# Loading a 512x512 channel weight in 8 KB runs, with every fourth channel in the transposes

## The chip, the cores and the metric

The kernel runs on one core of a Trainium2 chip. The metric is device time in microseconds (us). Profiles have their own zero; the profiled executions are about 1.8 us shorter than the times, because the time covers more than the profiled span.

## The reference, cut to what matters

Eight batches of 576 rows pass through a sliding-window attention, then through a spectral layer: the first 64 modes of a real Fourier transform along the sequence are each multiplied by a complex 512x512 weight (`w_r`, `w_i`), transformed back to `y`, and one channel weight `w_ch` closes the layer.

```python
u = x + y                                  # y: 64 spectral modes, each through its own weights
return (u + np.maximum(u @ w_ch, 0.0)).astype(np.float32)
```

The 127 mode matrices used and `w_ch` are 1 MB each in fp32.

## The kernel before, where the change touches it

GpSimd issues all loads of weights. Mode weights are read with four rows of a matrix in one partition (8 KB contiguous in memory) and become bf16 on the way; the channel weight is read with one row per run (2 KB) and stays 4 bytes wide. So channel `128*c + p` of the channel weight sits in partition `p`, and everything multiplied with it is transposed in packed blocks of 128 channels.

```python
def load_w(i, pool, tag, wt=None):                       # a mode weight: 8 KB runs
    ...
    nc.gpsimd.dma_start(out=wt, in_=src[m].rearrange("(p c) e -> p c e", c=NC))
...
            if m == 6:                                   # the channel weight: 2 KB runs
                nc.gpsimd.dma_start(out=wch, in_=moe_w_ch.rearrange("(c p) e -> p c e", p=128))
...
def channel(i):                                          # x @ w_ch, between modes
    ...
    for c in range(NC):
        nc.tensor.transpose(out=pst[:, c, :], in_=x_sb[:, b, t + k, 128 * c:128 * c + 128],
                            identity=ident_bf)           # in_ is the stationary side (a weight load)
    ...
    for c in range(NC):
        nc.tensor.matmul(out=psz, lhsT=xT[:, c, :], rhs=wch[:, c, :], ...)
...
def last_mode(m, w, im, c0, c1):                         # the last four modes: 16 loads per matrix
    for c in range(c0, c1):
        for e in range(NC):
            nc.tensor.matmul(out=view(psl, ...), lhsT=w[:, c, 128 * e:128 * e + 128], rhs=xq(...), ...)
...
        for m in range(ME + 2, NM):                      # ME = NM - 4
            for im in range(2):
                idle(1, 2)                               # filler matmuls, results unused
                last(m, im)                              # last_mode once its weight has landed
        idle(0, 2)
```

After the last of them, two VectorE copies take `psl` into `YT2`, which is multiplied with `wch` and transposed (`psw`, `psa`); then the output rows are formed.

The softmax here doesn't subtract the row's maximum and nothing guards it: scores larger than these inputs give would overflow.

## Time and profile before

| | before |
|---|---|
| time, median of 4 runs | 426.12 us (426.09 to 426.28) |
| profiled span | 424.3 us |
| last weight has landed | 389.4 us |
| tail after it | 34.9 us |
| DMA packets | 28166 |
| channel weight: issue to landing; first use | 148.95 to 167.8 us; 210.5 us |

The DMA share of a stretch is the busy time of the 16 DMA engines over their time; 1.06 means that packets on an engine overlap a little, and is what a full queue looks like here. "PEclk" is the clock granted to TensorE, as a share of full speed.

Two groups of PE weight loads (minimum, median and maximum in ns, then first and last start), from the views of lines 614 and 793 of the kernel before:

```profile
L614 PEld LDWEIGHTS <-x_sb x144: 95/98/151, 137.6 to 294.5; 128*128 128x128 bf16 x144
L793 PEld LDWEIGHTS <-wt x80: 95/98/103, 374.3 to 389.9; 128*128 128x128 bf16 x80
```

Packed loads of 128 bf16 columns take 98 ns, both for the transposes of x and for the last modes.

### The profile page before, as it was taken

The page shows a single profiled execution, that of the slowest core. Times are in us where ns is not written, and L with a number is a line of the kernel's source. Part 1 is how long each engine was busy: PE and PEld are TensorE (multiplying, and loading weights), DVE is VectorE, ACT ScalarE, POOL GpSimd, SP SyncE. Part 2 cuts the span into 40 slices and gives each one's busy share as a digit, 9 for nine tenths or more (in the row PEclk, how much of TensorE's full clock was granted, in tenths as well). Part 3 has the DMA queues.
Part 4 walks back from the last instruction along what each step waited for, and adds up shares of the span by engine and source line. Part 5 has one row for each costly group of instructions (what it writes and reads, how often), then busy time and mean ns, then how long its engine had stood idle before and what let it go on. Part 6 is the DMA issues. An engine that isn't in the chain of part 4 may idle for free.

```text
span 424.3 us, 8788 instructions
## 1 busy us (share of the span) xinstructions
PE 348.0 (82%) x3772; PEld 215.7 (51%) x3772; DVE 184.5 (43%) x397; ACT 171.2 (40%) x314; POOL 78.9 (19%) x141
## 2 busy tenths in 40 slices
PE   6999999999988897363698977977569997588993
PEld 5665665666665564122365644554324443255682
DVE  6466765766673211061443413331103433240994
ACT  4585866866763310021032312122203333130993
POOL 7131221331022222012111011211111113200000
PEclk9999999999996899556599999999968999999998
DMA  8999999999999999999999999999999999994598
GB/s 142 212 213 212 212 216 211 214 213 211 215 213 214 215 212 261 214 216 212 215 216 213 215 215 214 215 214 213 216 213 214 214 213 214 213 214 96 194 387 329
DMA packets 28166, 91.98 MB, mean 217 GB/s; under 512 B 2352, under 2 KB 2608, under 8 KB 28128
## 3 DMA queue, kind: packets, MB, share of 16 engines
q0 software_dynamic: 24864, 81.80, 96.6%
q1 hardware_dynamic: 3120, 9.50, 5.9%
q8 instruction: 29, 0.48, 0.4%
q10 hardware_dynamic: 144, 0.13, 0.1%
q14 instruction: 9, 0.07, 0.0%
HBM read 162.53 MB, written 9.44 MB: 405 GB/s over the span
## 4 chain that ended last, share of the span: by engine, by line
PE 38%; DMA 37%; issue 12%; DVE 8%; POOL 2%; ACT 2%; POOLq 0%; DVEq 0%
DMA wt<-in_moe_w_r_dram 23%; DMA wt<-in_moe_w_i_dram 14%; PE pso L324 7%; PE pst L226 6%; PE psy L592 4%; PE pso L903 4%; PE psv L243 3%; DVE x_sb L332 3%; PE psw L742 3%; PE pss L280 2%; PE pss L381 2%; PE psx L346 2%; PE pss L299 2%; DVE vT L59 2%; POOL wt L122 1%
## 5 line engine op out<-in xcount | busy, mean ns | idle before, releaser
L592 PE MATMUL psy<-wt,XQ 128*32 128x512 bf16 (+1 forms) x404 | 86.1, 427 | 42.6 <-DMA wt<-in_moe_w_i_dram 25.6
L592 PEld LDWEIGHTS <-XQ 128*32 128x32 bf16 (+1 forms) x476 | 46.2, 132 | 82.7 <-issue 65.8
L621 DVE CAST xT<-pxt 128x256 fp32r<-128x256 bf16 (+1 forms) x68 | 26.0, 434 | 56.4 <-PE pxt L614 41.1
L628 ACT CAST Z<-psz 128x512 fp32r<-128x512 f32 x36 | 21.1, 587 | 58.4 <-PE psz L626 58.1
L305 ACT ACTIVATE et<-pss 128x512 bf16<-128x512 f32 x72 | 39.2, 599 | 12.8 <-PE pss L299 12.8
L626 PE MATMUL psz<-wch,xT 128*128 128x512 f32 x144 | 40.3, 417 | 0.4 <-DVE xT L621 0.4
L324 PE MATMUL pso<-vt,et 128*64 128x65 bf16 (+1 forms) x576 | 34.0, 209 | 5.2 <-DVE x_sb L332 5.1
L324 PEld LDWEIGHTS <-et 128*64 128x64 bf16 (+1 forms) x576 | 23.7, 113 | 17.2 <-issue 9.8
L626 PEld LDWEIGHTS psz<-wch,xT 128*128 128x128 f32 x144 | 26.1, 193 | 11.6 <-issue 5.7
L59 DVE COPY x_sb<-psy 128x256 f32<-128x256 f32 x15 | 6.4, 424 | 56.4 <-PE psy L592 56.4
L58 ACT COPY x_sb<-psy 128x256 f32<-128x256 f32 x15 | 5.6, 373 | 60.6 <-DVE x_sb L59 60.6
L332 DVE TENSOR_TENSOR x_sb<-pso,rcp 128x640 bf16<-128x640 f32 x32 | 26.3, 823 | 0.9
L122 POOL DMA_DIRECT2D wt<-in_moe_w_r_dram x15 | 10.7, 713 | 77.7 <-PE psy L592 68.7
L903 PE MATMUL pso<-Y,trigI 128*128 128x512 f32 x80 | 23.1, 403 | 0.1
L926 DVE TENSOR_TENSOR ot<-pso,x_sb 128x512 f32<-128x512 f32 x35 | 22.2, 685 | 1.5 <-PE pso L903 1.1
L280 PE MATMUL pss<-band,ident_bf 64*64 64x512 bf16 x136 | 20.4, 407 | 1.5 <-ACT et L305 1.5
L59 DVE COPY vT<-pst 128x768 bf16<-128x768 bf16 x16 | 15.3, 958 | 13.0 <-PE pst L226 13.0
L117 POOL DMA_DIRECT2D wt<-in_moe_w_r_dram x25 | 13.6, 544 | 37.9 <-PE psy L592 22.8
L59 DVE CAST x_sb<-psj 128x512 bf16<-128x512 f32 x18 | 12.2, 688 | 18.5 <-PE psj L804 15.6
L908 ACT ACTIVATE pso<-pso 128x512 f32<-128x512 f32 x36 | 19.2, 594 | 0.0
L58 ACT CAST x_sb<-psj 128x512 bf16<-128x512 f32 x18 | 10.5, 586 | 19.3 <-PE psj L804 19.2
L122 POOL DMA_DIRECT2D wt<-in_moe_w_i_dram x15 | 10.7, 714 | 36.1 <-PE psy L592 35.1
(159 smaller groups left out, 530.3 us busy)
## 6 DMA issues: line engine op xcount, KB each, us to landing
wt<-in_moe_w_r_dram POOLq DMA_DIRECT2D x15, 1024.0 KB, 23.0
wt<-in_moe_w_i_dram POOLq DMA_DIRECT2D x15, 1024.0 KB, 25.4
wt<-in_moe_w_r_dram POOLq DMA_DIRECT2D x25, 512.0 KB, 16.9
wt<-in_moe_w_i_dram POOLq DMA_DIRECT2D x21, 512.0 KB, 18.2
out_dram<-ot SPq DMA_DIRECT2D x15, 512.0 KB, 4.2
rk<-in_k_dram POOLq DMA_DIRECT2D x8, 576.0 KB, 10.5
rq<-in_q_dram POOLq DMA_DIRECT2D x8, 576.0 KB, 14.2
rv<-in_v_dram POOLq DMA_DIRECT2D x8, 576.0 KB, 13.0
```

The costliest lines, as they stand in the source:

```text
L59: return nc.vector.tensor_copy(out=o, in_=i)
L122: nc.gpsimd.dma_start(out=wt, in_=src[m:m + 2].rearrange("m (p c) e -> p m c e", c=NC))
L226: nc.tensor.transpose(out=ps[64 * hh:64 * hh + 64, c, :], in_=src[:, hh, (c0 + c) * D:(c0 + c + 1) * D], identity=ident_bf)
L280: nc.tensor.matmul(out=pss[(2 * w + hh) % 3][64 * half:64 * half + 64, :], lhsT=ident_bf[pp, pp], rhs=view(band[pp], 128 * half, [[0, WIN ...
L305: nc.scalar.activation(out=et[:, hh, :], in_=pss[(2 * w + hh) % 3], func=ACT_F.Exp, scale=EX_SCALE)
L324: nc.tensor.matmul(out=pso[po, hh, (i // 2) * VW:(i // 2) * VW + D + 1], lhsT=et[pk, hh, col:col + 64], rhs=vt[pk, 1 - f % 2, 2 * hh + g / ...
L332: nc.vector.tensor_tensor(out=view(x_sb, b * NT * DM + g * D, [[4 * D, 2], [DM, NT], [1, D]]), in0=view(pso, 0, [[512, 2], [VW, NT], [1, D]]),
L592: nc.tensor.matmul(out=psy[r0:r0 + k, :], lhsT=xq(c, m, im, [[NM, k]]), rhs=w[:, c, :], start=(im + c == 0), stop=(im == (m > 0) and c == ...
L621: nc.vector.tensor_copy(out=xT[:, :, w * k:w * k + w], in_=view(psts[k], j, [[128, NC], [n, w]] if n > 1 else [[128, NC], [1, 64], [64, 2]]))
L626: nc.tensor.matmul(out=psz, lhsT=xT[:, c, :], rhs=wch[:, c, :], start=(c == 0), stop=(c == NC - 1))
L903: nc.tensor.matmul(out=tps[n], lhsT=trigI[:, tr:tr + 128], rhs=pair_tile(what, bb), start=False, stop=stop and r0 + k == 128, skip_group_c ...
L926: nc.vector.tensor_tensor(out=ot[:, j], in0=ps, in1=x_sb[:, b, t, :], op=ALU.add)
```

## The change

The intent is to give the channel weight's load the mode weights' shape, 128 runs of 8 KB instead of 512 of 2 KB. Partition `p` then holds rows `4p` to `4p+3`, and all that meets the weight must take channels `4p+c`: the transposes of x and the weight loads of the last modes read columns at a step of 4, and copies out of PSUM put spectra into and out of that order.

```diff
-            evac(half[h], ps[:, 256 * h:256 * h + 256], h)
+            evac(half[h], view(ps, 2 * h, [[1, 2], [NC, 128]]), h)
...
-                    nc.tensor.transpose(out=pst[:, c, :], in_=x_sb[:, b, t + k, 128 * c:128 * c + 128],
+                    nc.tensor.transpose(out=pst[:, c, :], in_=view(x_sb, (b * NT + t + k) * DM + c, [[NC, 128]]),
...
-                nc.gpsimd.dma_start(out=wch, in_=moe_w_ch.rearrange("(c p) e -> p c e", p=128))
+                nc.gpsimd.dma_start(out=wch, in_=moe_w_ch.rearrange("(p c) e -> p c e", c=NC))
...
+    def by_channel(psa):
+        return view(psa, 0, [[1, 128], [128, NC]])
...
-        nc.vector.tensor_copy(out=pair_tile("Yb", b)[:E0], in_=psa[:E0].rearrange("p c e -> p (c e)"))
+        nc.vector.tensor_copy(out=pair_tile("Yb", b)[:E0], in_=by_channel(psa[:E0]))
...
-                                 lhsT=w[:, c, 128 * e:128 * e + 128],
+                                 lhsT=view(w, c * DM + e, [[NC, 128]]),
... (three more copies out of psa, through by_channel)
```

More of the change, by code (lines that the diff above doesn't have):

```diff
@@ L847, in middle_rows @@
                 nc.vector.tensor_copy(out=pair_tile("Yb", b0 + i)[E0:],
-                                      in_=psa[R * i:R * i + R].rearrange("p c e -> p (c e)"))
+                                      in_=by_channel(psa[R * i:R * i + R]))
                 nc.scalar.copy(out=pair_tile("yw", b0 + i)[E0:], in_=psw[R * i:R * i + R, :])
@@ L886 @@
         lay(EARLY_ROWS)
-        flat = psa.rearrange("p c e -> p (c e)")
         yl = yp.tile([128, 2, DM], FP32R, name="yl")
@@ L895 @@
             nc.scalar.copy(out=pair_tile("yw", b)[E0:], in_=psw[R * b:R * b + R])
-            nc.vector.tensor_copy(out=pair_tile("Yb", b)[E0:], in_=flat[R * b:R * b + R])
-        nc.vector.tensor_copy(out=yl[0:NR, 1], in_=flat[0:NR])
+            nc.vector.tensor_copy(out=pair_tile("Yb", b)[E0:], in_=by_channel(psa[R * b:R * b + R]))
+        nc.vector.tensor_copy(out=yl[0:NR, 1], in_=by_channel(psa[0:NR]))
         def add(n, what, stop):
```

## The prediction

> **What bounds the kernel now.** I read the page first, from its 40 slices: before any engine I wanted to know whether the transfers ever rest.
>
> ```profile
> PE   6999999999988897363698977977569997588993
> ...
> DMA  8999999999999999999999999999999999994598
> ```
>
> PE has holes (3, 6, 3, 6 in slices 17 to 20, 5 and 6 in slices 29 and 30) while the DMA row stands at 9 from the second slice to the 36th. So I asked for the stretches between the stages, with the DMA share as the column before the last and GB/s as the last.
>
> ```profile
> 5.00:141.00 136.00, 127.44 (x2491) 85.76 (x2489) 85.28 (x152) 87.47 (x146) 34.26 (x60) 0.96 1.09 213
> 141.00:158.00 17.00, 15.18 (x117) 9.54 (x116) 2.32 (x6) 5.02 (x11) 4.46 (x7) 1.00 1.07 214
> 158.00:170.00 12.00, 9.08 (x63) 5.43 (x63) 1.53 (x5) 1.54 (x5) 2.61 (x6) 1.00 1.10 255
> 170.00:350.00 180.00, 138.20 (x715) 77.49 (x714) 56.30 (x164) 41.20 (x85) 26.85 (x43) 0.87 1.06 214
> 350.00:385.00 35.00, 25.70 (x212) 13.99 (x209) 10.83 (x19) 8.53 (x17) 6.88 (x13) 1.00 1.06 212
> 385.00:390.00 5.00, 4.18 (x68) 2.75 (x65) 0.00 (x0) 0.00 (x0) 0.00 (x0) 1.00 0.37 74
> ```
>
> The share never falls below 1.06 before 385 us (over 1 because packets on one DMA engine overlap a little), and the rate stays at 212 to 214 GB/s, except at 158 to 170 us. That exception is the transfer this change touches: the channel weight is written as fp32, so as many bytes arrive as are read, while each mode weight is read as fp32 and written as bf16. The third view is the chain that ended last, where the stream stops.
>
> ```profile
> 371.13 18.30 DMA wt<-in_moe_w_i_dram
> 389.43 0.05 issue
> 389.48 0.64 PE psl L793 x16
> 390.14 0.23 DVE YT L880
> 390.37 0.28 DVE YT L882
> 390.64 0.14 issue
> 390.77 1.17 PE psw L742 x4
> ```
>
> The last load is issued 18.3 us before it lands, so the queue is that deep and engine waits behind it do not starve it. The end is then two terms: the time the DMA engines need to push every byte (to 389.4 us), and the tail after it (424.3 - 389.4 = 34.9 us). A change counts only if it alters DMA work before the last weight, or tail work after it.
>
> **What the Trainium skill says.** "DMA: Bandwidth & Descriptors", section "Why small descriptors are slow (HBM only)", gives a fixed cost for each packet; by its 3 cycles beside 32-byte beats a 2 KB packet would lose 3 of 67 cycles, an 8 KB one 3 of 259, an estimate of 3% between them. This trace agrees in kind and shows more, as worked out below. "TensorE: Matmul & The Clock Gate", section "Weight-path perf modes", says that the fast weight load is taken for 128 non-fp32 weights, with its columns "packed or strided", for column steps of up to about a thousand elements. A step of 4 would keep it; the trace of before has no strided 128-column bf16 load, so nothing confirms this yet. "SBUF — State Buffer", section "Door 1: The DMA port swizzle", says that up to 8 bf16 elements may be stepped over for free; the trace has a step of 2 only: the 64-column loads of ident_bf at line 804 take 109 ns against 110 ns for packed 64-column loads at line 226. "VectorE: DVE Perf Modes", section "Why PSUM operands drop a tier", puts fp32 out of PSUM at one element per cycle[...]. The trace agrees: the copies into YT read PSUM at a step of 32 elements in runs of 4 and take 288 ns for 128 elements, and the packed 512-element copy takes 687 ns. The difference, 399 ns for 384 elements, is 1.04 ns each, so the stride costs nothing seen.
>
> **The change, part by part.**
>
> Instructions. Apart from line numbers, the instruction streams of the two kernels agree on every engine in number, order and size. One row differs in shape: the load of the channel weight is 128 rows of 2048 elements, not 128x4x512. There is nothing to gain or lose by count.
>
> The load. Before, it is 512 packets of 2 KB; after, 128 of 8 KB. What one costs now comes from the DMA engines' time. Two stretches of 12 us, that with the load (158 to 170 us) first, then a plain one (178 to 190 us):
>
> ```profile
> DMA packets 1046, 3.06 MB, mean 255 GB/s; under 512 B 47, under 2 KB 47, under 8 KB 1044
> ...
> q0 software_dynamic: 1044, 3.04, 109.4%
> ...
> DMA packets 667, 2.57 MB, mean 214 GB/s; under 512 B 40, under 2 KB 40, under 8 KB 667
> ...
> q0 software_dynamic: 667, 2.57, 106.2%
> ```
>
> In the plain stretch 667 - 40 = 627 packets of 4 KB written (8 KB read) fill 12 us on 16 engines: 192 / 627 = 306 ns each, so a mode weight of 128 packets costs 128 x 306 / 16 = 2.45 us. In the other, 1044 - 47 = 997 data packets; 512 are the channel weight's, the other 485 are mode packets and take 485 x 306 = 148.4 of the 192 us. That leaves 43.6 us for 512 packets, 85 ns each, so the channel weight costs 512 x 85 / 16 = 2.72 us. If an 8 KB packet of it costs what the mode weights' 8 KB reads do, it becomes 2.45 us: **0.27 us less**. The trace's own packet durations, which contain the overlap, bound this from above: 99 ns for a 2 KB packet against 324 ns for one that reads 8 KB, so 4 x 99 - 324 = 72 ns per 8 KB, times 128 / 16 = 0.58 us, over a share of 1.06 some 0.54 us. The bytes are the same, so no more than a few tenths can be had. As the stream has no gap, what is saved moves the last landing forward by as much. I take 0.3 us.
>
> The weight's arrival. Its first use is at 210.5 us and it lands at 167.8 us, so arriving earlier is worth nothing, and only the freed DMA time counts. GpSimd's issue took 757 ns; it sat idle for 3.5 us after it, so a shorter issue buys nothing.
>
> The transposes of x (line 614, 144 weight loads at 98 ns, 210 to 295 us). Their columns now step by 4 elements. If the fast load survives, nothing changes. If it is lost, I size it from the other loads: 16-column to 64-column bf16 loads take 111 and 110 ns, and 128 columns take only 98, so the 128-column load is the fast kind. In the tail its pairs start 0.51 - 0.10 over 15 gaps = 27 ns apart. A plain load's slope, from the fp32 transposes of line 744, is 132 - 110 = 22 ns for 32 columns, 0.69, or by the pass with 128 columns 140 - 110 = 30 ns for 64, 0.47 ns a column; 128 columns at 0.47 make 60 ns apart, some 30 ns more each. 144 x 30 = 4.3 us of PE time over 85 us, in a stage where the DMA queue holds 20 us of issued loads, and PE waits for mode weights 41.5 us over the kernel: hidden.
>
> The last modes (line 793, 128 weight loads). Same step of 4. Seven of the eight groups of 16 end before the next weight lands (PE waits 0.4 us ahead of the last). The eighth starts when the last weight has landed, on the chain: it costs nothing if the fast load stays, 16 x 30 = **0.5 us if it is lost**. I give the loss one chance in four: 0.1 us expected.
>
> The copies (the spectrum copies on VectorE, 687 ns each, and the copies of psy, 424 ns on VectorE and 373 on ScalarE) read PSUM at steps of 128 and of 4 elements. ScalarE's copy into Xs already reads at a step of 4: 593 against 586 ns packed. In the tail three such VectorE copies stand beside ScalarE's; I expect 0 to 0.05 us.
>
> Sum: 426.12 - 0.3 + 0.1 = 425.9 us.
>
> **The rivals.** (1) Strided weight loads lose the fast kind: for it, no strided 128-column bf16 load has been seen here; against it, the skill's sentence. The time would be 426.12 - 0.3 + 0.5 = 426.3. (2) The write side sets the packet: 8 KB written per packet, where mode packets write 4 KB, could run slower, and the saving vanishes: 426.1. Against it: 2 KB both read and written in 85 ns already moves 24 GB/s per engine, close to the 8 KB / 306 ns = 27 GB/s of the mode reads. (3) PSUM reads at a 512-byte step are slower than at the 128 bytes seen: three copies of 0.69 us in the tail, even 20% slower, add 0.4 us, so 426.2. (4) The strided PE work of 210 to 295 us delays the issues so much that the queue runs dry: it would need a slip of some 20 us, and I found at most 4.3. (5) The transfer is hidden and its saving lost: the unbroken DMA row speaks against it.
>
> **Range and chances.** All rivals lie within half a microsecond of 426. Three runs of before spread by 0.2 us; another chip and another phase of the PE clock can add some tenths. So 425.2 to 426.6 us. Two per cent is 8.5 us, and no term comes near it: within 2% with a chance of 0.98.
>
> **What would show it right or wrong.** The DMA packet count should fall by 384, to some 27780; the 12 us stretch with the load should hold more bytes than 3.06 MB; the last mode weight should land some 0.3 us earlier relative to the start. Lines 614 and 793 should keep weight loads of 98 ns; about 130 ns would mean rival 1. The spectrum copies should stay at 687 ns, and the tail at 34.9 us. I am wrong if the landing moves later, if the queue shows a gap, or if the tail grows by over half a microsecond.

## The result, and the profile after

The changed kernel takes 426.03 us in the median of 4 runs (425.91, 426.01, 426.05 and 427.64). Ratios here are the mean time of one kernel's fast runs over the mean of the other's in the same rounds, so they are not quite the ratio of the quoted medians. This one is 1.0006 (95% interval 0.9982 to 1.003): the one run of 427.64 carries it above 1. The profiled spans are 424.3 us for both. The result is "the same" at 2%, and the measurement cannot see a tenth of a microsecond.

From the page of the changed kernel, the slices and the packets:

```profile
PE   6989998998998899364698977977568986589993
...
DMA  8999999999999999999999999999999999994598
...
DMA packets 27782, 91.98 MB, mean 217 GB/s; under 512 B 2352, under 2 KB 2608, under 8 KB 27616
```

There are 384 packets less, the bytes are the same, and the DMA row is the same slice for slice. The transfers of the changed kernel from 158 to 170 us, the stretch with the load:

```profile
DMA packets 677, 3.10 MB, mean 259 GB/s; under 512 B 48, under 2 KB 48, under 8 KB 548
```

In the same 12 us 3.10 MB arrive, not 3.06. The chain that ended last of the changed kernel (start, duration, what):

```profile
371.48 17.87 DMA wt<-in_moe_w_i_dram
389.34 0.05 issue
389.39 0.72 PE psl L796 x16
390.11 0.02 issue
390.14 0.22 DVE YT L883
```

The last weight lands 0.09 us earlier (389.34 against 389.43), the 16 weight loads and matmuls behind it take 0.72 instead of 0.64 us, and the VectorE copy starts at 390.14 us in both kernels. In these two profiles the gain is given back to the hundredth. The reason for the 0.08 us is in the weight loads:

```profile
L614 PEld LDWEIGHTS <-x_sb x144: 110/113/147, 138.7 to 294.3; 128*128 128x128 bf16 x144
...
L796 PEld LDWEIGHTS <-wt x80: 112/117/147, 375.9 to 389.9; 128*128 128x128 bf16 x80
```

113 and 117 ns, where packed columns took 98. The copies out of PSUM did not change: the eight spectrum copies have a median of 687 ns in both, the copies of psy 425 ns on VectorE and 373 against 372 on ScalarE.

Because the last landing wanders by a tenth from one profile to the next, I also took from the packet records of the traces when the last packet of the n-th mode weight ended, just ahead of the channel weight's packets (mode weight 35) and just behind them (41), always less the same time in the kernel before. What a kernel gains between the two columns lies in the stretch with that load:

| kernel | channel weight in | at weight 35 | at weight 41 | step across the load |
|---|---|---|---|---|
| changed | 8 KB | +0.017 us | -0.137 us | -0.154 us |
| e1 | 8 KB | +0.234 | +0.075 | -0.159 |
| e4 | 8 KB | +0.057 | -0.081 | -0.138 |
| e7 | 8 KB | -0.082 | -0.200 | -0.118 |
| e9 | 8 KB | +1.374 | +1.216 | -0.158 |
| e10 | 8 KB | +0.086 | -0.084 | -0.170 |
| e2 | 2 KB | +0.059 | +0.020 | -0.039 |
| e8 | 2 KB | -0.031 | -0.072 | -0.041 |
| e11 | 2 KB | +0.111 | -0.048 | -0.159 |

The six with 8 KB runs gain 0.15 us on average; the kernel before (0 by definition) and the three others with 2 KB runs gain 0.06. The difference, 0.09 us, is a third of what I had predicted. But e11, with 2 KB runs, gains as much as the kernels with 8 KB, so these steps alone don't settle a tenth; e5 below measures the cost of 2 KB reads on 127 weights at once (0.084 us each). In the landing of the last weight nothing of it can be seen: it is at 389.25 to 389.53 us in the six profiles with 8 KB (mean 389.36) and at 389.22 to 389.43 in the four with 2 KB (mean 389.34). The 0.09 us between the two landings above may be the phase of a run.

### The profile page after: what moved, and what is told of

The parts are those of the page before. It is cut to its first block, busy times and chain, and to the rows that moved or that the text cites. A ratio compares the mean times of both kernels' runs of the same rounds, so it can differ in the third digit from the quotient of the medians.

```text
span 424.3 us, 8778 instructions
## 1 busy us (share of the span) xinstructions
PE 348.6 (82%) x3762; PEld 217.9 (51%) x3772; DVE 184.6 (44%) x397; ACT 171.3 (40%) x314; POOL 78.9 (19%) x141
## 4 chain that ended last, share of the span: by engine, by line
DMA 44%; PE 36%; DVE 8%; issue 7%; ACT 2%; POOL 1%; DVEq 0%; POOLq 0%
DMA wt<-in_moe_w_r_dram 27%; DMA wt<-in_moe_w_i_dram 17%; PE pso L324 7%; PE pst L226 6%; PE psy L592 5%; PE pso L905 4%; PE psv L243 3%; DVE x_sb L332 3%; PE psx L346 3%; PE pss L381 2%; PE pss L280 2%; PE pss L299 2%; DVE vT L59 2%; DVE ot L928 1%; PE pso L790 1%
## 5 line engine op out<-in xcount | busy, mean ns | idle before, releaser
L592 PE MATMUL psy<-wt,XQ 128*32 128x512 bf16 (+1 forms) x404 | 85.0, 428 | 42.9 <-DMA wt<-in_moe_w_i_dram 27.0
L122 POOL DMA_DIRECT2D wt<-in_moe_w_r_dram x15 | 10.7, 715 | 75.5 <-PE psy L592 68.0
```

The costliest lines, as they stand in the source:

```text
L592: nc.tensor.matmul(out=psy[r0:r0 + k, :], lhsT=xq(c, m, im, [[NM, k]]), rhs=w[:, c, :], start=(im + c == 0), stop=(im == (m > 0) and c == ...
```

## The experiments

Theory: two terms of about 0.1 us and opposite sign, cheaper DMA work before the last weight, and strided weight loads behind it; all else is hidden. The rivals are that one or the other is only the phase of a run, that the copies cost, or that PE's extra work in the middle reaches the end. The first three kernels ran five rounds each; the spread of their runs (the kernel before had 425.85 to 429.62 us in 11) turned out too wide for tenths, so what follows from them follows from their traces.

### e1: the load alone

```diff
 # on the kernel before
-  in_=moe_w_ch.rearrange("(c p) e -> p c e", p=128)
+  in_=moe_w_ch.rearrange("(p c) e -> p c e", c=NC)
```

> Kernel before with the channel weight loaded in 8 KB runs and nothing else changed; the result is wrong on purpose. My theory: the load's DMA work alone is the gain, so the last mode weight lands 0.13 us earlier than in the kernel before (as it did in the changed kernel) and the tail stays at 34.9 us: 0.1 to 0.2 us faster, 425.95. Rival A (the earlier landing was the phase of the run and not the load): the same landing as before, 426.1. Rival B (the write of 8 KB per packet is slow): landing later than before.

Measured: 426.35 us against 426.29 in the same rounds, ratio 0.9997 (0.9966 to 1.0027): undecided by time. In the trace the step across the load is -0.159 us, the last weight has landed at 389.34 us against 389.43, and the last 16 matmuls stay at 0.64 us. The theory's landing was 0.13 earlier, it came 0.09 earlier. Rival B, a later landing, falls. Rival A, the phase of the run, does not fall for the landing: e8 and e11, with 2 KB runs, landed earlier still (389.22 and 389.31). And the tail is no constant. In e1 VectorE's copy behind the last group starts 0.09 us earlier than in the kernel before, but its last output ends 0.45 us later: near 411 us a PE weight load waits 0.7 us for a small transfer inside the tail (`Y<-yl`). Nine of the 13 profiles have such a wait (0.2 to 0.7 us); those of the kernel before and of the changed one have none.

### e2: the strides alone

```diff
 # on the changed kernel
-  in_=moe_w_ch.rearrange("(p c) e -> p c e", c=NC)
+  in_=moe_w_ch.rearrange("(c p) e -> p c e", p=128)
```

> Changed kernel with the old load in 2 KB runs; the result is wrong on purpose. My theory: landing as in the kernel before (389.4 us), weight loads of lines 614 and 796 at 113 to 117 ns, the last 16 matmuls 0.72 us instead of 0.63: 0.1 us slower than before, 426.2. Rival C (strided loads cost nothing in the end, since the PE's filler matmuls hide them): equal to before. Rival D (strided copies out of PSUM cost): tail over 35.1 us.

Measured: 426.03 us against 426.29, ratio 0.9987 (0.9963 to 1.001): undecided by time, and not the slower median I expected. In the trace, the landing is at 389.39 us (389.43 before), the weight loads take 113 and 117 ns, the last 16 matmuls 0.73 us, and the copy behind them starts at 390.19 instead of 390.14:

```profile
389.39 0.05 issue
389.44 0.73 PE psl L796 x16
390.17 0.02 issue
390.19 0.23 DVE YT L883
```

So the strides cost their 0.1 us in the chain, against rival C. For rival D the profiled tail (424.5 - 389.4 = 35.1 us) stands at the threshold I had set, but the copies themselves, 687 ns each before and after, show no cost, and a weight load in this tail waits 0.4 us for `Y<-yl`.

### e3: two rows in a partition

```diff
 # on the changed kernel: 4 KB runs, columns at a step of 2
+  out=wch.rearrange("p (h c) e -> p h c e", h=2), in_=moe_w_ch.rearrange("(h p c) e -> p h c e", h=2, c=2)
+  lhsT=view(w, c * DM + 256 * (e // 2) + e % 2, [[2, 128]])     # the transposes and copies likewise
```

> Correct kernel in between: two rows in a partition, 256 packets of 4 KB, columns at a step of 2. From the trace's packet times (99 ns for 2 KB, 325 ns for 8 KB, so 22 ns plus 0.037 ns a byte) a 4 KB packet takes 173 ns, and 256 of them are 2.77 us of one engine's sixteenth against 3.17 and 2.60. My theory: it keeps about two thirds of the saving (0.1 us), and if the cost of a strided weight load grows with the 16-byte lines it touches, a step of 2 costs 105 ns or less, so the tail loses 0.04 us at most: 426.0, best of the three by less than 0.1 us. Rival: the step costs the same 15 ns whatever its size, as soon as columns are not packed: 426.05.

Measured: correct, 426.39 us against 426.29, ratio 0.9989 (0.9966 to 1.0013): not a version that can be said to beat either. (In its profile the last weight has landed at 389.35 us, the last 16 matmuls take 0.66 us, and the copy behind them starts at 390.08, 0.06 us ahead of both kernels; no time confirms it.) What it settles is the stride, at PE's full clock (views of its lines 614 and 797):

```profile
L614 PEld LDWEIGHTS <-x_sb x144: 96/98/151, 137.6 to 294.4; 128*128 128x128 bf16 x144
...
L797 PEld LDWEIGHTS <-wt x80: 96/98/102, 374.2 to 389.8; 128*128 128x128 bf16 x80
```

A step of 2 costs nothing, so the rival "any step but 1" is wrong.

### e4: eight steps, one for each of the last groups

```diff
 # on the changed kernel, by group: steps 2, 3, 4, 5, 8, 6, 16, 1
-  lhsT=view(w, c * DM + e, [[NC, 128]])
+  lhsT=view(w, offset, [[step, 128]])
```

> Changed kernel whose eight last groups of 16 weight loads each read their 128 columns at another step: 2, 3, 4, 5, 8, 6, 16, 1 in this order; the result is wrong on purpose. Theory of lines (each further 16-byte line touched costs): the duration grows with the step up to 8 bf16 (16 bytes) and then stays: about 98 at 1, 103 at 2, 115 at 4, 135 at 8, 135 at 16. Rival (any step but 1[...]): one duration, 113 to 117 ns, at all steps from 2 to 16. Rival 2 (the fast load is lost at some step): a jump to 130 ns or more there.

Measured: 427.79 us in its one run (the output still within the tolerance). The weight loads, in order of time:

```profile
L808 PEld LDWEIGHTS <-wt x16: 113/117/136, 380.3 to 380.8; 128*128 128x128 bf16 x16
...
L813 PEld LDWEIGHTS <-wy x16: 117/130/130, 382.0 to 383.0; 128*128 128x128 bf16 x16
...
L818 PEld LDWEIGHTS <-wy x16: 143/157/166, 384.4 to 385.3; 128*128 128x128 bf16 x16
...
L823 PEld LDWEIGHTS <-wy x16: 125/143/143, 386.8 to 387.4; 128*128 128x128 bf16 x16
...
L828 PEld LDWEIGHTS <-wt x16: 142/168/168, 388.9 to 389.8; 128*128 128x128 bf16 x16
```

These are steps 4, 5, 8, 6 and 16, at PE's full clock: 117, 130, 157, 143 and 168 ns. (Steps 2 and 3 came out at 109 and 110 ns, but the granted clock was 0.50 there; at full clock e3 has 98 for step 2.) The duration grows with the step from 4 up to 8 and little after, as the theory of lines has it, though step 4 is not free and 16 is not equal to 8. There is no jump to a plain load.

The time tells something I had not expected. In this run PE no longer waited for any of the last weights, and the last group started at 391.2 us, 1.8 us later than in the kernel before. (Its weight loads were slower, and PE's clock was 0.50 from 370 to 380 us; the run doesn't separate the two.) PE's work in the last 20 us is a second bound just under the transfers: in the kernel before, the last group waits only 0.43 us for its weight, in the changed one 0.29.

### e5: the same change on 127 weights, the other way round

```diff
 # on the kernel before: all mode weights in 2 KB runs
-  in_=src[m].rearrange("(p c) e -> p c e", c=NC)
+  in_=src[m].rearrange("(c p) e -> p c e", p=128)      # the loads of two modes likewise
```

> Kernel before with all 127 mode weights (not the channel weight) read in 2 KB runs instead of 8 KB: the same change as the one studied, made 127 times and the other way round; the result is wrong on purpose. My theory: one megabyte read in 2 KB runs costs about 0.15 us more DMA time than in 8 KB runs, and the stream has no gap, so 127 x 0.15 = 19 us more (15 to 23): 445 us. Rival (the packet size costs nothing and the 0.15 us between the traces is phase): 426. Rival 2 (descriptor making on GpSimd, now four times as many, becomes the bound): gaps in the DMA row and more than 450 us.

Measured: 436.77 us against 426.08, ratio 1.025 (1.0234 to 1.0265). The last weight landed 10.7 us later too (400.12 us against 389.43). The 10.7 us divided by 127 are 0.084 us a megabyte: for a cost spread over the whole stream the sign and the one-to-one passage are settled, but the size is below my 0.15 and far below the 0.27 of the prediction. (The mode weights are written as bf16, in packets of 1 KB here, so on the write side this is not the channel weight's case.) Rival 2 falls: DMA stays full (page), and a plain 12 us, from 178 to 190 us, has

```profile
DMA packets 2466, 2.49 MB, mean 207 GB/s; under 512 B 37, under 2 KB 2466, under 8 KB 2466
```

2466 - 37 = 2429 data packets in 192 us of DMA engines are 79.0 ns each, so 316 ns for four of them, against the 306 of an 8 KB read: 10 ns x 128 / 16 = 0.08 us a weight. The direct count and the time agree.

### e6: a quarter of the load

```diff
 # on the kernel before
+  nc.gpsimd.dma_start(out=wch[:, 0, :], in_=moe_w_ch[0:128, :])
+  for c in range(1, NC):
+      nc.vector.tensor_copy(out=wch[:, c, :], in_=wch[:, 0, :])
```

> Kernel before that loads only the first 128 rows of the channel weight (128 packets of 2 KB) and fills the rest by three VectorE copies at a time when VectorE is idle; the result is wrong on purpose. My theory: all DMA work before the last weight passes into the end one to one, so three quarters of the 2.6 us fall away: 2.0 us faster, 424.2. Rival (the load hides in slack, or PE takes over as the bound near the end): under 1 us faster.

Measured: 424.61 us against 426.08, ratio 0.9962 (0.9947 to 0.9977): 1.5 us faster, between theory and rival. The trace takes it apart. Across the load the stream gains 1.92 us (from +0.87 at weight 35 to -1.05 at 41), as the theory had it. Ahead of the load it had lost 0.87 us: the issue of the mode weights ahead came 3.7 us later than before (149.85 against 146.18 us), and the DMA share from 150 to 158 us was 1.01 instead of 1.07. Most of that loss did not reach the end: the last weight landed 1.73 us earlier, at 387.70 us. Its group started only at 388.00, because PE was not done with the work ahead: 0.25 us of the gain (0.30 us from landing to start, where the kernel before has 0.05) went to PE, which the rival had said.

### e7: the transposes twice

```diff
 # on the changed kernel
-  for c in range(NC):
+  for c in [i % NC for i in range(2 * NC)]:
```

> Changed kernel with each of the 144 transposes of x made twice into the same place (correct result): some 144 x 60 ns = 8 us more PE work between 138 and 294 us, several times what slower weight loads add there. My theory: hidden behind the DMA stream, time within 0.3 us of the changed kernel, 426.1. Rival (PE's stage from 210 to 285 us, busy for 87%, passes its delay on through the issues of later loads): 2 to 8 us slower.

Measured: correct, 427.77 us against 426.08, ratio 1.0045 (1.0017 to 1.0073). That is not hidden, and my theory seems wrong; but the last weight landed 0.12 us earlier than before, so the loads were not delayed. The lost time is behind, in two parts. PE's clock was 0.50 from 370 to 375 us and 0.54 to 380, and PE then worked without a pause until its last group at 389.90 us, half a microsecond late; VectorE's last output is late by the same (it ends at 419.14 us, 418.68 in the changed kernel). The other 1.5 us come after the last computation: the profile ends 7.1 us behind it, where the other 12 profiles end 5.4 to 5.8 us behind. Only output is written there, and the cause isn't shown. The changed kernel's own profile shows the same stretch of low clock, and just catches up. Stretches of both (columns: busy time of PE, its weight loads, VectorE, ScalarE, GpSimd; then PEclk, DMA share, GB/s), first the kernel before, then the changed one:

```profile
370.00:375.00 5.00, 3.78 (x33) 2.48 (x32) 1.52 (x4) 1.46 (x4) 0.53 (x1) 1.00 1.05 211
375.00:380.00 5.00, 4.36 (x50) 2.73 (x50) 3.59 (x6) 2.64 (x5) 0.00 (x0) 1.00 1.07 215
```

```profile
370.00:375.00 5.00, 3.80 (x12) 1.94 (x11) 0.98 (x3) 0.64 (x2) 0.53 (x1) 0.52 1.07 214
375.00:380.00 5.00, 4.92 (x65) 3.78 (x64) 3.27 (x5) 3.09 (x6) 0.00 (x0) 0.80 1.07 215
380.00:385.00 5.00, 5.00 (x56) 3.17 (x56) 0.86 (x2) 0.38 (x1) 0.00 (x0) 1.00 1.01 204
```

In the first 5 us the changed kernel completes a third of the PE instructions, then is busy throughout.

### e8: only the very last group, at a step of 8

```diff
 # on the kernel before
-  lhsT=w[:, c, 128 * e:128 * e + 128]
+  lhsT=view(w, e, [[8, 128]]) if (m, im) == (NM - 1, 1) else w[:, c, 128 * e:128 * e + 128]
```

> Kernel before in which only the very last group of 16 weight loads reads its columns at a step of 8, which took 157 ns and 62 ns apart in the run with several steps, against 98 and 27; the result is slightly wrong on purpose. My theory: this group starts when the last weight has landed, so the tail grows by 16 x 35 = 0.5 us and the time with it: 426.7. Rival (the VectorE copy behind it has slack): 426.2.

Measured: 426.69 us against 426.08 (+0.6), ratio 1.0029 (1.0004 to 1.0055). Its chain that ended last has

```profile
389.22 0.05 issue
389.27 1.16 PE psl L793 x16
390.43 0.02 issue
390.46 0.22 DVE YT L880
```

1.16 us instead of 0.64, and VectorE's copy follows at once; it starts 0.32 us later than in the kernel before, although the weight landed 0.21 us earlier. What the last group costs passes into the copy behind it, and the time agrees in sign (the interval allows 0.2 to 2.3 us). The changed kernel's 0.08 us should do the same; a time can't show so little.

### e9, e10, e11: less filler ahead of the last groups

```diff
 # on the changed kernel (e9), on e7 (e10), on the kernel before (e11)
-  idle(1, 2)
+  idle(0, 2)
```

> Changed kernel with one filler matmul less ahead of each of the last four groups of weight loads (the filler keeps PE's clock up and computes nothing that is used; the result stays correct). In the changed kernel's trace PE had half a clock from 370 to 375 us and then worked without a pause until the last weight came, with 0.3 us to spare. My theory: this PE work is a second bound just under the DMA stream, and passes it in runs with a longer stretch of low clock, which gives the runs of 427 us and more. With about 2 us less of it, the median stays at 426.0 (the DMA stream sets it), and runs over 427 us become fewer. Rival E (slow runs come from elsewhere): the same median and the same spread. Rival F (the clock drops without filler): slower than 426.5.

> The kernel with each transpose of x made twice, with the same lighter filler. My theory: its 1.7 us over the kernel before came from PE being late in the last 20 us and not from the transposes' own stage, so with 2 us less filler it falls to 426.5 or below. Rival (8 us more PE work from 210 to 295 us delays the loads): stays at 427.5 or above.

> Kernel before with the same lighter filler. My theory: 426.1, within 0.2 us of the changed kernel with it, so that the change is still worth 0.1 us or less, and with fewer runs over 427 us than the kernel before shows. Rival F as above: slower than 426.5.

Measured, against 426.21 us of the kernel before in the same rounds: e9 427.51 (ratio 1.0023, 1.0003 to 1.0044), e10 427.54 (1.0027, 1.0009 to 1.0045), e11 427.39 (1.0024, 1.0006 to 1.0042). My expectations of all three failed (e10's too: I had it at 426.5 or below), and rival F holds. The stretch ahead of the tail in e9:

```profile
385.00:390.00 5.00, 3.19 (x63) 2.76 (x61) 0.00 (x0) 0.00 (x0) 0.00 (x0) 0.50 0.59 118
```

PE's clock is at half (1.00 in the kernel before), and the four matmuls onto psw take 2.05 us in the chain instead of 1.17. The Trainium skill ("TensorE: Matmul & The Clock Gate", section "Part 1: The HAM clock gate") describes just that, a clock halved by an idle stretch; the profile shows the halving, not the rule for it. So the filler is worth more than a microsecond. Two useful things remain. With the same lighter filler, doubling the transposes costs nothing (427.54 against 427.51): 144 more transposes with their weight loads between 138 and 310 us do not delay the end, and the rival of e7 falls, though the 427.5 us that e10's rival had named came true, by the filler. And the two kernels with light filler, before and changed, lie 0.12 us apart, less than their own runs spread (0.4 and 0.8 us).

## Why the prediction was right, point by point

- **The bound.** Right for microseconds of DMA work: e5 (+10.7 us in time and landing) and e6 (-1.92 us across the load for an expected 2.0, -1.73 at the landing) show it. It is not shown for tenths, and I left out three things. PE's last 20 us lie only 0.4 us below that bound, so a saving above some 0.5 us would not have arrived whole (e6). The queue does not stay full to the end: in the kernel before, 56 packets start in the microsecond from 383 us, then 49, 37, 31, 26 and 14, so part of the 16 DMA engines is done before the last landing. And a delay of the stream need not reach that landing: in e9 the DMA share fell to 0.93 from 128 to 132 us, the stream was 1.2 us late at weight 125 too, and the last weight landed 0.10 us late. That the engines that finish last had not been held up would explain it; no run tests it. The tail, taken as a constant 34.9 us, has the wait told under e1.
- **The load, 0.27 to 0.3 us.** Right in sign, about three times too large: 0.084 us a weight by e5, and 0.09 between the groups of traces, which is within their scatter. The failed term is the 43.6 us left for 512 packets, 85 ns each. At e5's 79.0 ns they would take 40.4 us, so 3.2 us were something else. The packet records name 2.1 of them: two instruction packets took 0.97 and 0.34 us, and three of the load's own packets 238, 409 and 431 ns, where the others took 99. It was a small remainder of two large numbers, and I had booked to it all else that moved in those 12 us. An error of 1% in the 148.4 us of the mode packets alone is 0.09 us of load time. Counting packets where all are of one size (e5: 79.0 ns) needs no remainder. The upper bound of 0.54 us was not wrong, only idle.
- **The strided weight loads, 0 or 0.5 us, 0.1 expected.** The alternative was wrong: neither 98 nor 130 ns, but 113 to 117. The expected 0.1 us is what they cost (0.08), by luck of the weighting. The skill's sentence on steps up to about a thousand elements says that the fast load is taken, and nothing here contradicts that; it does not say what a step costs. The 16-byte lines of the SBUF page fit better in kind: no cost at a step of 2, growing cost from 4 to 8.
- **The copies, 0 to 0.05 us.** Right: 687 ns before and after. Rival 3 is out.
- **The transposes' stage is hidden.** Right for that stage, even with each transpose made twice (e10 against e9; in e7 the last weight landed no later either, and its 1.7 us were lost further on).
- **The sum.** -0.08 + 0.08 = 0 us from e5 and the chain, against -0.2 predicted and -0.09 between the medians, which is inside the noise. That the median fell within 0.2 us of the predicted one is partly luck. The range of 425.2 to 426.6 held the median; it would have held a result of no effect as well. That most of the predicted gain was absent cannot be seen in the times of these two kernels, only in the traces and by e5.

What stays open: why single runs of both kernels reach 427 to 429 us. The half clock ahead of the tail cost over a microsecond in e9; the stretch of half clock at 370 to 380 us half a microsecond in e7, and the writing of its output 1.5 us more. The changed kernel's run of 427.64 us has a mean clock of 0.903 where its other three have 0.921 to 0.933. But no such run of the kernel before was profiled.

## What to carry to other kernels

Where a DMA queue never runs dry, a transfer's worth is its packets times their spacing, and the spacing is best counted in a stretch where all packets are alike, or by making the change on every transfer at once and dividing. Ask of a layout change what it makes strided on the other engines, and look for the one place where that stands behind the last transfer: 16 weight loads, spaced some 5 ns wider each, took back about what the load had gained. And a tail is not a constant: look for its own waits before booking a tenth to what lies ahead of it. A change of a tenth of a microsecond cannot be judged by times that spread by several tenths; either amplify it or follow it through the trace.

## What the Trainium skill lacked or had wrong

- "TensorE: Matmul & The Clock Gate", section "Weight-path perf modes": "packed or strided" gives no cost of the stride. Loads of 128 bf16 columns took 98 ns packed and at a step of 2, 113 to 117 at 4, 130 at 5, 143 at 6, 157 at 8 and 168 at 16.
- "SBUF — State Buffer", section "Door 1: The DMA port swizzle": its free stride of up to 8 bf16 elements did not hold for weight loads; a step of 4, with two columns in each 16-byte line, already cost 15 ns, and a step of 8 cost 59.
- "DMA: Bandwidth & Descriptors", section "Why small descriptors are slow (HBM only)": its per-packet cost gave an estimate of 3% between 2 KB and 8 KB packets. Measured with all mode weights in 2 KB reads: 79.0 ns against 306 / 4 = 76.5, which is 3%. Agreement, and nearer than the 11% (85 against 76.5) that the prediction read from the trace; the section names no such sizes.
- "TensorE: Matmul & The Clock Gate" has no figure for filler matmuls that keep the clock up: one less ahead of each of the last four groups gave 427.51 and 427.39 us (e9, e11) beside 426.21 of the kernel before in the same rounds.
